# Where the sums of w_in's magnitudes are taken: in the decoding, or later from its high halves

## The chip, the cores and the metric

The kernel runs on one core of a Trainium2 chip. The core has TensorE (PE, with its weight loads PEld), VectorE (DVE), ScalarE (ACT), GpSimd (POOL) and SyncE (SP), each working through its own queue strictly in order, and 16 DMA engines that all queues share. The metric is the device time of one execution in microseconds; the time before is the median of three runs.

## The reference

```python
attn_out = _attn_ref(q, k, v)            # 4 batches, 8 heads, 576 tokens, width 64; the 32 largest scores of a row are kept
x = attn_out.transpose(0, 2, 1, 3).reshape(2304, 512)
h = x @ w_in                             # 512 x 2048
g = np.maximum(h, 0.0) + np.log1p(np.exp(-np.abs(h)))
x = g @ w_out                            # 2048 x 512
# then a layer of 8 experts: each token goes to the expert with the largest logit
ye = np.maximum(xe @ w1[e], 0.0) @ w2[e]
out[mask] = gate_w[mask, None] * ye
```

q, k, v, w_in and w_out arrive as 64-bit numbers; the kernel reads their bits as pairs of 32-bit words where it has to.

## The kernel before

Part one does attention and the first dense layer together, part two the experts. Attention is worked in 72 groups of two score tiles (128 rows by 576). For a group, TensorE makes the scores in two pieces (sa, sb), ScalarE copies them into s (lines 416 and 452), VectorE finds the 32nd largest value of each row (lines 446 to 472), ScalarE copies it to kths (line 479), masks and takes the exponential (480, 482), GpSimd subtracts (481, 491, 492), and SyncE transposes the result by DMA (494) for the product with v.

The dense layer is worked in ten units of one or two tiles of 128 tokens, each in 16 steps over the width of 2048. A step multiplies by a block of w_in (line 596), takes exponential and logarithm (610, 611), and multiplies by a block of w_out (636). For the last two units the step also splits its factors into two halves (lines 614 to 617, which call `halves`, 622 and 623). The fourth unit to start is the one of a single tile, tail0.

w_in and w_out are decoded at the start: 32 calls of `decode` or `decode_w_in`, two ahead and four per group, each of 128 x 512 numbers. `decode_w_in` gets a float32 tile t, takes the sum of its magnitudes (line 258; the result itself is scratch, only the sum, w_sums, is kept), makes the high half in float16 (259) and the low half (260). The sums are used much later: `check`, in part two, tests that each lies between 64 and 60000, to decide whether the whole must be done again with scaling.

The program is written group by group, and a scheduler then sets the order on each engine. It places an instruction by priority and by when it could start in a timeline of its own, so an instruction with nothing left to wait for may come far ahead of the place where it is written. A tile name has a fixed number of buffers; t has one (`DCB = 1`), the raw q, k and v tiles have one each (`RB = 1`), so that a new load of vn waits for the last use of the old. Line 335 takes sums over q, k and v as well.

Of the kernel before, what the change touches and what calls it, by code (L numbers as in the profile page):

```python
# [8 lines left out]
F32 = mybir.dt.float32  # L9
# [4 lines left out]
AF = mybir.ActivationFunctionType  # L14
# [10 lines left out]
KD = DM // 128  # L25
# [24 lines left out]
UNITS = [[(b,2*i),(b,2*i+1)] for b in range(3) for i in range(2)]+[[(0,'tail0')],[(3,0),(3,1)],[(3,2),(1,'tail1')],[(3,3)]]  # L50
# [13 lines left out]
C = 512  # L64
# [136 lines left out]
def part_one(tc, ctx, q, k, v, w_in, w_out, const, ident, before, ones, iota_e, reg_e, wg, ids,  # L201
             ohcum, done, early, table, rows, flags, sums, w_sums, e_sums, kths):
    nc = tc.nc
    late = []

    def pool(name, bufs, **kw):
        return ctx.enter_context(tc.tile_pool(name=name, bufs=bufs, **kw))
# [5 lines left out]
    dec = pool("dec", DCB)  # L213
# [12 lines left out]
    w_in_s = wp.tile([128, KD, DFF // C, 2, C], F16, name="w_in_s")  # L226
# [9 lines left out]
    def decode(src, kk, c0, dst):  # L236
        w = dec.tile([128, 2 * C], I32, name="w", bufs=DWB)
        nc.sync.dma_start(w, src[:, kk, 2 * c0:2 * (c0 + C)])
        w = w.rearrange("p (a b) -> p a b", b=2)
        hi, lo = w[:, :, 1], w[:, :, 0]  # L240
        a = x2p.tile([128, ROWW], F32, name="xr")[:, :C]

        decoded[0] += 1
        b = ps_y.tile([128, DM], F32, name="y") if decoded[0] <= DEC_PS else a
        nc.scalar.activation(b, hi.bitcast(F32), AF.Copy, scale=2.0 ** -111)
        u, v = a.bitcast(U32), b.bitcast(U32)
        nc.vector.tensor_scalar(v, v, 3, None, op0=ALU.logical_shift_left)

        nc.scalar.activation(lo, lo.bitcast(U32), AF.Copy, scale=2.0 ** -29)
        nc.vector.scalar_tensor_tensor(u, hi.bitcast(U32), 0x80000000, v, op0=ALU.bitwise_and, op1=ALU.bitwise_or)
        nc.gpsimd.tensor_tensor(out=dst.bitcast(I32), in0=a.bitcast(I32), in1=lo, op=ALU.add)

    def decode_w_in(kk, j):
        t = dec.tile([128, C], F32, name="t")
        decode(w_in_v, kk, j * C, t)
        nc.scalar.activation(w_in_s[:, kk, j, 1], t, AF.Abs, accum_out=w_sums[:, j, kk:kk + 1])
        nc.scalar.activation(w_in_s[:, kk, j, 0], t, AF.Copy)
        nc.gpsimd.tensor_tensor(out=w_in_s[:, kk, j, 1], in0=t, in1=w_in_s[:, kk, j, 0], op=ALU.subtract)  # L260

# [38 lines left out]
    for j in range(DFF // C):  # L300
        if flags is None:
            dec_q += [(decode, w_in_v, kk, j * C, w_in_f[:, kk, j]) for kk in range(KD)]
            dec_q += [(split_w_in, j)]
        else:
            dec_q += [(decode_w_in, kk, j) for kk in range(KD)]
        dec_q += [(decode, w_out_v, kk, c0, w_out_s[:, kk, c0:c0 + C])
                  for kk in range(j * C // 128, (j + 1) * C // 128) for c0 in range(0, DM, C)]
# [256 lines left out]
    def moe_step():  # L564

        if not cur and ready:
            cur.append(Unit(*ready.pop(0)))
        if cur:
            u = cur[0]
            if u.x is None:  # L570
                u.x = unit_x(u.tiles)
            layer1(u)
            behind.append((u, u.f))
            u.f += 1
            if u.f == KF - XAHEAD and ready:
                cur.append(Unit(*ready.pop(0)))
                cur[1].x = unit_x(cur[1].tiles)
            if u.f == KF:
                cur.pop(0)
        if behind and (not cur or len(behind) > GLAG):  # L580
            layer2(*behind.pop(0))

    def layer1(u):
        f, n, (xT, hs, dn) = u.f, 128 * len(u.tiles), u.x
        hps = ps_h.tile([128, 512], F32, name="h")
        j, o = divmod(f * 128, C)
        if hs is None:
            down = 2.0 ** (-8 - X_UP)
        else:
            down = hs[:, j:j + 1]  # L590
            if o == 0:
                nc.vector.tensor_scalar(down, w_inv[:, j:j + 1], dn, None, op0=ALU.mult)
        m = 0
        for c in range(KD):
            for p, r in ((0, 0), (0, 1), (1, 0)):
                nc.tensor.matmul(hps[:, :n], lhsT=w_in_s[:, c, j, p, o:o + 128], rhs=xT[:, 0:len(u.tiles), r, c, :],  # L596
                                 start=m == 0, stop=m == 3 * KD - 1)
                m += 1
        a = ep.tile([128, 256], F32, name="sa")
        g = gp.tile([128, 256], F32, name="g")[:, :n]  # L600
        if flags is None:
            nc.scalar.activation(a[:, :n], hps[:, :n], AF.Abs, scale=down)
            nc.scalar.activation(g, hps[:, :n], AF.Relu, scale=down)
            nc.scalar.activation(a[:, :n], a[:, :n], AF.Exp, scale=-1.0)
            nc.scalar.activation(a[:, :n], a[:, :n], AF.Ln, bias=1.0)
            nc.gpsimd.tensor_tensor(out=g, in0=g, in1=a[:, :n], op=ALU.add)
        else:

            k = (u.number - 1) * KF + f
            nc.scalar.activation(a[:, :n], hps[:, :n], AF.Exp, scale=down, accum_out=e_sums[:, k:k + 1])  # L610
            nc.scalar.activation(g, a[:, :n], AF.Ln, bias=1.0)  # L611
        if u.number >= TAIL:

            g2 = raw.tile([128, R * D], F32R, name="qkv"[f % 3] + "n")[:, :2 * n].rearrange("p (s t) -> p s t", s=2)
            halves(g2, g)
            w2 = dec.tile([128, 2 * C], F32R, name="w", bufs=DWB).rearrange("p (s c) -> p s c", s=2)
            halves(w2, w_out_s[:, f, :])
            g = g2, w2
        u.g[f] = g

    def halves(t, src):
        nc.scalar.activation(t[:, 0], src, AF.Copy)
        nc.vector.tensor_tensor(out=t[:, 1], in0=src, in1=t[:, 0].bitcast(F32), op=ALU.subtract)
# [168 lines left out]
    for i in range(-1, n + LAG):  # L792
# [28 lines left out]
        j = i - LAG  # L821
# [284 lines left out]
```

## Time and profile before

| | us |
|---|---|
| median of three runs | 1065.49 (1062.65 to 1066.71) |
| the profiled execution | 1060.82, span 1059.1 |
| busy: PE, DVE, ACT, POOL | 889.8, 853.0, 801.3, 603.0 |
| line 258, activation, 16 times | 0.616 each |
| 19th and 23rd copy of kths | at 224.59 and 263.99 |
| last copy of kths | at 703.2 |

The profile is one execution. Busy time is the time in which an engine ran an instruction; an engine that isn't busy waits for another engine, for a transfer or for its own sequencer. Since every engine takes its instructions in order, one that waits holds back all that stand behind it.

### The profile page before, as it was taken

What the parts mean: (1) busy time and instruction counts of PE and PEld (TensorE: products, weight loads), DVE (VectorE), ACT (ScalarE), POOL (GpSimd) and SP (SyncE); (2) the same over time, 40 slices, a digit from 0 to 9 for tenths busy, and PEclk for the clock granted to TensorE, in tenths of its full rate; (3) what the DMA queues carried; (4) which work ended last, traced back from release to release, by engine and by line L of the source; (5) the groups of instructions that cost most, each with busy time, mean ns of one, the idle gap of its engine ahead of it and who ended that gap; (6) DMA issues with size and microseconds to landing.
All of it is one profiled execution on the core that took longest, in us unless ns stands there. A gap on an engine that the chain in (4) does not pass through costs nothing.

```text
span 1059.1 us, 22197 instructions
## 1 busy us (share of the span) xinstructions
PE 889.8 (84%) x7146; PEld 659.0 (62%) x7146; DVE 853.0 (81%) x3021; ACT 801.3 (76%) x1866; POOL 603.0 (57%) x631
## 2 busy tenths in 40 slices
PE   1124379666989797998999999999999999999994
PEld 0012256344656565665666667666787999999993
DVE  5789999899988688997889999965357987777774
ACT  5889899888799678897998898863677655555553
POOL 3889898998678587776877877762001022111111
PEclk9986579777999989998999999999999999999998
DMA  7897898985889987659876755564301667766760
GB/s 189 202 216 165 201 202 176 200 173 100 129 117 171 124 131 136 108 85 150 156 155 113 116 85 98 80 93 124 112 11 32 164 214 240 246 221 220 234 213 24
DMA packets 295859, 156.97 MB, mean 148 GB/s; under 512 B 257524, under 2 KB 257652, under 8 KB 295732
## 3 DMA queue, kind: packets, MB, share of 16 engines
q1 hardware_dynamic: 292116, 145.73, 65.2%
q0 software_dynamic: 3616, 9.72, 2.6%
q8 instruction: 58, 0.95, 0.4%
q14 instruction: 69, 0.57, 0.2%
HBM read 77.89 MB, written 11.11 MB: 84 GB/s over the span
## 4 chain that ended last, share of the span: by engine, by line
PE 47%; DVE 13%; DMA 9%; ACT 8%; POOL 6%; issue 4%; SPq 1%; POOLq 0%; ACTq 0%; DVEq 0%
PE h L937 10%; PE y L950 9%; PE h L596 9%; PE y L636 8%; DVE mx L472 3%; PE y L633 3%; DVE wk L468 3%; POOL e L481 2%; DMA vn<-in_v_dram 2%; DMA kt<-st 2%; DMA pT<-p 2%; PE m L509 1%; PE sb L406 1%; POOL p L492 1%; ACT e L482 1%
## 5 line engine op out<-in xcount | busy, mean ns | idle before, releaser
L636 PE MATMUL y<-w_out_s,g 128*128 128x512 f32 x480 | 233.7, 610 | 5.3 <-ACT g L611 4.7
L596 PE MATMUL h<-xT,w_in_s 128*128 128x256 f16 (+1 forms) x1920 | 224.5, 267 | 9.1 <-POOL w_in_s L260 3.2
L596 PEld LDWEIGHTS <-w_in_s 128*128 128x128 f16 x1920 | 173.6, 100 | 70.2 <-issue 43.6
L481 POOL TENSOR_TENSOR e<-s,e 128x576 f32<-128x576 f32 x144 | 202.5, 1421 | 16.9 <-ACT e L480 16.5
L472 DVE MAX8 mx<-wk 128x8 f32<-128x128 f32 (+2 forms) x432 | 200.8, 500 | 0.1
L492 POOL TENSOR_TENSOR p<-e,p 128x512 f16<-128x512 f32 x144 | 167.3, 1162 | 0.0
L406 PEld LDWEIGHTS <-q 128*128 128x128 f16 (+1 forms) x640 | 56.1, 109 | 175.5 <-issue 127.6
L468 DVE MATCH_REPLACE8 wk<-mx,wk 128x128 f32<-128x128 f32 (+1 forms) x432 | 144.6, 341 | 0.1
L636 PEld LDWEIGHTS y<-w_out_s,g 128*128 128x128 f32 x480 | 83.7, 195 | 69.0 <-issue 57.6
L917 POOL DMA_INDIRECT out_dram<-ot,idx x19 | 19.5, 1028 | 175.7 <-DVE ot L916 172.9
L482 ACT ACTIVATE e<-e,bias 128x576 f32<-128x576 f32 x144 | 110.5, 768 | 11.0 <-POOL e L481 10.4
L406 PE MATMUL sa<-kt,q 128*128 128x256 f16 (+1 forms) x320 | 53.0, 305 | 77.0 <-DMA kt<-st 22.9
L937 PEld LDWEIGHTS h<-xT,wf 128*128 128x128 f32 x864 | 111.8, 191 | 5.3 <-ACT wf L898 0.2
L937 PE MATMUL h<-xT,wf 128*128 128x256 f32 x864 | 113.9, 283 | 0.0
L950 PE MATMUL y<-wf,hT 128*128 128x512 f32 x432 | 112.8, 398 | 0.0
L406 PE MATMUL sb<-kt,q 128*128 128x320 f16 (+1 forms) x320 | 63.1, 340 | 50.9 <-ACT s L452 50.8
L480 ACT ACTIVATE e<-s,kths 128x576 f32<-128x576 f32 x144 | 105.0, 766 | 0.9
L509 PEld LDWEIGHTS <-pT 128*128 128x128 f16 (+1 forms) x1440 | 88.2, 107 | 24.4 <-issue 18.3
L509 PE MATMUL m<-v,pT 128*128 128x65 f16 (+1 forms) x1440 | 95.2, 202 | 9.5 <-DVE x L536 4.9
L490 ACT ACTIVATE p<-e 128x576 f16<-128x576 f32 x144 | 97.4, 678 | 5.0 <-DMA pT<-p 4.3
L491 POOL TENSOR_TENSOR p<-e,p 128x64 f16<-128x64 f32 x144 | 46.1, 320 | 73.6 <-ACT p L490 72.2
L610 ACT ACTIVATE sa<-h 128x256 f32<-128x256 f32 (+1 forms) x160 | 56.3, 352 | 40.1 <-PE h L596 39.3
(213 smaller groups left out, 1817.1 us busy)
## 6 DMA issues: line engine op xcount, KB each, us to landing
w1r<-in_moe_w_dram SPq DMA_DIRECT2D x20, 1024.0 KB
w2r<-in_moe_w_dram SPq DMA_DIRECT2D x20, 1024.0 KB, 6.6
w<-in_moe_w_in_dram SPq DMA_DIRECT2D x16, 512.0 KB, 4.2
w<-in_moe_w_out_dram SPq DMA_DIRECT2D x16, 512.0 KB
rows<-xr SPq DMA_DIRECT2D x37, 128.2 KB, 2.7
qn<-in_q_dram SPq DMA_DIRECT2D x16, 288.0 KB, 3.6
kn<-in_k_dram SPq DMA_DIRECT2D x16, 288.0 KB, 3.1
vn<-in_v_dram SPq DMA_DIRECT2D x16, 288.0 KB, 4.7
```

Of the source, the lines that this page charges most:

```text
L406: last_qk[0] = nc.tensor.matmul(ps[p0:p1], lhsT=qs[:, h, r0:r1, :].rearrange("p r d -> p (r d)"), rhs=kt[:, k0:k1, cs], start=first, stop= ...
L468: nc.vector.match_replace(out=to, in_to_replace=mx[:, i, 8 * j:8 * j + 8], in_values=src[i], imm_value=NEG)
L472: nc.vector.max(out=mx[:, i, 8 * j + 8:8 * j + 16], in_=src[i])
L480: nc.scalar.activation(e[i], s[i], AF.Relu, bias=kths[:, 2 * gi + i], scale=-K_UP)
L481: nc.gpsimd.tensor_tensor(out=e[i], in0=s[i], in1=e[i], op=ALU.subtract)
L482: nc.scalar.activation(e[i], e[i], AF.Exp, bias=bt[:, i], scale=SCORE)
L492: nc.gpsimd.tensor_tensor(out=p16[:, S + D:], in0=e[i][:, 0:S - D], in1=p16[:, 0:S - D], op=ALU.subtract)
L509: nc.tensor.matmul(o[:, h, 0:D + 1], lhsT=pT(r), rhs=v16[:, h, c, 0:D + 1], start=r == 0, stop=r == R - 1)
L596: nc.tensor.matmul(hps[:, :n], lhsT=w_in_s[:, c, j, p, o:o + 128], rhs=xT[:, 0:len(u.tiles), r, c, :], start=m == 0, stop=m == 3 * KD - 1)
L636: nc.tensor.matmul(u.y[i], lhsT=g[:, cs], rhs=w_out_s[:, f, :], start=f == 0, stop=f == KF - 1)
L937: nc.tensor.matmul(h, lhsT=w1f[:, a, c, :], rhs=xT[:, b, c, :], start=n == 0, stop=n == 3 * KD - 1)
L950: nc.tensor.matmul(y[i], lhsT=hT[g][:, a, i * 128:i * 128 + 128], rhs=w2f[:, b, :], start=g == 0 and n == 0, stop=g == KF2 - 1 and n == 2)
```

## The change

The sum over t in `decode_w_in` goes. In its place the step f of unit 8 takes, behind the place where the last two units split their factors, one sum of the high half that block (wj, wk) of w_in has in float16, with wj and wk counted by f, so that the 16 steps give the same 16 sums of magnitudes, now of rounded numbers. The scratch result goes to a tile t of the same single buffer as the decoding's.

```diff
     def decode_w_in(kk, j):
         t = dec.tile([128, C], F32, name="t")
         decode(w_in_v, kk, j * C, t)
-        nc.scalar.activation(w_in_s[:, kk, j, 1], t, AF.Abs, accum_out=w_sums[:, j, kk:kk + 1])
         nc.scalar.activation(w_in_s[:, kk, j, 0], t, AF.Copy)
         nc.gpsimd.tensor_tensor(out=w_in_s[:, kk, j, 1], in0=t, in1=w_in_s[:, kk, j, 0], op=ALU.subtract)
...
             halves(w2, w_out_s[:, f, :])
             g = g2, w2
+        if flags is not None and u.number == len(UNITS) - 2:
+            t, (wj, wk) = dec.tile([128, C], F32, name="t"), divmod(f, KD)
+            nc.scalar.activation(t, w_in_s[:, wk, wj, 0], AF.Abs, accum_out=w_sums[:, wj, wk:wk + 1])
         u.g[f] = g
```

Lines 259 to 617 of the kernel before are one lower in the new one, lines from 618 on two higher; the new sum is line 620. The scheduler's order changes with it, on all engines. Three places of ScalarE follow, each before and then after.

Before, at the last tile of w_in that is decoded (t is the decoded tile, w_in_s its halves, w and xr the next tile of w_out):

```order
L452 ACTIVATE s<-sb 128x2x320
L458 ACTIVATE bias<-mx 128x2
L258 ACTIVATE w_in_s,w_sums<-t 128x512
L259 ACTIVATE w_in_s<-t 128x512
L482 ACTIVATE e<-e,bias 128x576
L247 ACTIVATE xr<-w 128x512
L251 ACTIVATE w<-w 128x512
```

After, at the same tile, up to the first two of the new sums:

```order
L489 ACTIVATE p_2495<-e 128x576
L258 ACTIVATE w_in_s<-t 128x512
L247 ACTIVATE xr<-w 128x512
L251 ACTIVATE w<-w 128x512
...
L478 ACTIVATE kths<-mx 128x2
L489 ACTIVATE p_2501<-e 128x576
L479 ACTIVATE e<-s,kths 128x576 x2
L620 ACTIVATE t,w_sums<-w_in_s 128x512
L609 ACTIVATE sa,e_sums<-h 128x256
L247 ACTIVATE xr<-w 128x512
L251 ACTIVATE w<-w 128x512
L609 ACTIVATE sa,e_sums<-h 128x256
L620 ACTIVATE t,w_sums<-w_in_s 128x512
```

The sum ahead of the high half is gone, and the new sums begin a few rows behind the last high half; all 16 stand within the next 72 rows, between the 19th and the 23rd copy of kths.

Before, at the sum over vn of the eleventh pair of heads (q_5384 is its scratch, vn the loaded tile), in group 34:

```order
L610 ACTIVATE sa,e_sums<-h 128x256
L611 ACTIVATE g<-sa 128x256
L666 ACTIVATE x2T<-h 128x512
L335 ACTIVATE q_5384,sums<-vn 128x576
L482 ACTIVATE e<-e,bias 128x576
L479 ACTIVATE kths<-mx 128x2
L482 ACTIVATE e<-e,bias 128x576
L416 ACTIVATE s<-sa 128x2x256
L367 ACTIVATE st<-kn 128x9x64
```

After, at the same sum:

```order
L668 ACTIVATE x2T<-h 128x512
L457 ACTIVATE bias<-mx 128x2
L610 ACTIVATE g<-sa 128x256
L481 ACTIVATE e<-e,bias 128x576
L489 ACTIVATE p_4692<-e 128x576
L415 ACTIVATE s<-sa 128x2x256
L334 ACTIVATE q_5368,sums<-vn 128x576
L609 ACTIVATE sa,e_sums<-h 128x256
L489 ACTIVATE p_4698<-e 128x576
L478 ACTIVATE kths<-mx 128x2
```

The copy of scores s, the exponentials e and one copy to p stood behind the sum over vn and now stand ahead of it.

Before, where the unit of one tile begins (xh is the input of a unit, split; 128x128 marks the steps of this unit), around the 39th copy of kths:

```order
L490 ACTIVATE p_5469<-e 128x576
L556 ACTIVATE xh<-x_4371 128x512
L479 ACTIVATE kths<-mx 128x2
L480 ACTIVATE e<-s,kths 128x576 x2
L610 ACTIVATE sa,e_sums<-h 128x128 x2
L611 ACTIVATE g<-sa 128x128 x2
L452 ACTIVATE s<-sb 128x2x320
```

After, around the 40th copy of kths:

```order
L489 ACTIVATE p_5587<-e 128x576
L555 ACTIVATE xh<-x_4355 128x512
L478 ACTIVATE kths<-mx 128x2
L479 ACTIVATE e<-s,kths 128x576 x2
L609 ACTIVATE sa,e_sums<-h 128x128
L610 ACTIVATE g<-sa 128x128
L609 ACTIVATE sa,e_sums<-h 128x128
```

The first steps of this unit, and the split of the unit after it, come one group later.

## Rows read from the trace of the kernel before

**Rows 1.** The page's busy tenths in 40 slices.
```profile
PE   1124379666989797998999999999999999999994
DVE  5789999899988688997889999965357987777774
ACT  5889899888799678897998898863677655555553
```
**Rows 2.** Busy us by stage: stretch, length, then each engine, PEclk, DMA share, GB/s.
```profile
50.00:224.60 174.60, 95.47 (x834) 62.18 (x834) 160.43 (x517) 154.29 (x329) 158.95 (x155) 0.76 0.89 195
224.60:264.00 39.40, 29.81 (x254) 20.41 (x255) 37.17 (x129) 33.15 (x74) 33.09 (x35) 0.78 0.58 120
370.10:440.00 69.90, 62.43 (x543) 43.05 (x543) 59.39 (x244) 55.89 (x141) 53.37 (x58) 0.89 0.75 132
440.00:703.20 263.20, 255.74 (x2315) 173.89 (x2314) 244.38 (x1012) 231.89 (x564) 200.00 (x213) 0.99 0.67 111
703.20:822.00 118.80, 117.28 (x915) 88.34 (x913) 60.61 (x275) 75.92 (x228) 19.03 (x22) 1.00 0.32 74
```
**Rows 3.** Line 258's instructions: ns min/median/max, first and last start.
```profile
L258 ACT ACTIVATE w_in_s<-t x16: 613/616/630, 12.7 to 218.2; 128x512 f16<-128x512 f32 x16
L258 ACT ACTIVATION_READ_ACCUMULATOR w_in_s<-t x16: 185/188/198, 13.2 to 218.7; 128x1 f32 x16
```
**Rows 4.** ACT in order of time: start us, duration us, instruction, idle before it.
```profile
16.61 0.63 ACT L258 ACTIVATE w_in_s<-t 128x512 f16<-128x512 f32 x1 [2.02 <-POOL t L253]
...
205.92 0.66 ACT L247 ACTIVATE xr<-w 128x512 f32<-128x512 f32 x1 [1.57 <-DMA w<-in_moe_w_in_dram]
...
209.64 0.67 ACT L335 ACTIVATE q<-vn 128x576 f16<-128x576 f32 x1
...
210.31 0.76 ACT L482 ACTIVATE e<-e,bias 128x576 f32<-128x576 f32 x1
210.97 0.61 ACT L258 ACTIVATE w_in_s<-t 128x512 f16<-128x512 f32 x1
...
211.58 0.61 ACT L259 ACTIVATE w_in_s<-t 128x512 f16<-128x512 f32 x1
212.10 0.19 ACT L479 ACTIVATE kths<-mx 128x2 f32<-128x2 f32 x1
...
224.59 0.19 ACT L479 ACTIVATE kths<-mx 128x2 f32<-128x2 f32 x1
...
263.99 0.20 ACT L479 ACTIVATE kths<-mx 128x2 f32<-128x2 f32 x1
```
**Rows 5.** DVE's waits in 50 to 224.6: us in total, times, longest.
```profile
DVE sb L446 <- ACT s L416: 7.4, 5, 2.9
...
DVE xr L249 <- ACT xr L247: 1.6, 1, 1.6
DVE y L249 <- ACT y L247: 0.8, 2, 0.5
```
**Rows 6.** ACT around the stall at 359, in order of time.
```profile
358.92 0.58 ACT L666 ACTIVATE x2T<-h 128x512 f32<-128x512 f32 x1
367.40 0.68 ACT L335 ACTIVATE q<-vn 128x576 f16<-128x576 f32 x1 [7.90 <-DMA vn<-in_v_dram]
...
369.51 0.57 ACT L416 ACTIVATE s<-sa 128x512 f32<-128x512 f32 x1
```
**Rows 7.** DVE behind the same stall.
```profile
370.11 0.43 DVE L446 TENSOR_TENSOR sb<-sb,s 128x256 f32<-128x256 f32 x1 [9.47 <-ACT s L416]
```
**Rows 8.** SP's queue ahead of it, in order of time.
```profile
355.10 1.59 SPq L702 DMA_DIRECT2D rows<-xr  x2
356.78 0.54 SPq L326 DMA_DIRECT2D vn<-in_v_dram  x1
```
**Rows 9.** PE by line and shape, 370 to 470: count, busy us, mean ns.
```profile
L636 PE MATMUL y<-w_out_s,g 128*128 128x512 f32 x73 | 38.6, 640 | 2.3 <-ACT g L611 2.2
L596 PE MATMUL h<-xT,w_in_s 128*128 128x128 f16 x192 | 13.0, 219 | 0.5 <-DMA xT<-xh 0.5
```

## The prediction

> **What bounds the kernel now.** I read the page's slices first, then a table of busy time by stage, then the groups of the lines that the change touches, then who waits for whom, and last the instructions around the longest stall. In the slices [rows 1] the reader is to see that no engine is free while attention runs: from the second slice to the 26th VectorE and ScalarE both stand at 6 to 9 tenths, mostly 8 and 9, and TensorE, low at first, is at 9 in most slices from the 11th on and from the 20th on in all but the last. The stage table [rows 2] puts numbers on this. While the weights are decoded, from 50.0 to 224.6 us, VectorE is busy 160.43 of 174.60 us (92%), GpSimd 158.95 (91%), ScalarE 154.29 (88%) and TensorE only 95.47 (55%). From 440.0 to the last softmax at 703.2, TensorE is busy 255.74 of 263.20 (97%) and VectorE 244.38 (93%). After that TensorE has no room left (117.28 of 118.80 up to 822). So the end is set by how soon attention gets through its 72 groups, with VectorE and ScalarE taking turns, and then by a fixed stretch of matmuls. Up to the last softmax both orders have the same number of unit steps behind them (117 exponentials of line 610), so that the stretch behind it is the same length, and a microsecond won or lost before it comes out at the end.
>
> **What is taken away.** Sixteen sums of line 258. One is an activation of 616 ns and a read of the accumulator of 188 ns [rows 3]. They overlap with what follows, so I take the price from the starts of one sum and its successor: 210.97 to 211.58, 0.61 us of ScalarE's queue [rows 4]. The first two, at 12.7 and 16.61 us, come where ScalarE waits for GpSimd's t in any case (2.02 us before the second), and the copy of line 259 takes over that wait: nothing there. The other fourteen are 14 x 0.61 = 8.5 us of the 154.29 that ScalarE is busy in the decoding. What can this bring? Not more than what VectorE waits for ScalarE there, 7.4 + 1.6 + 0.8 = 9.8 us [rows 5], and nothing if those waits come from transfers further up (line 247 itself waits 1.57 us for its weights at 205.92, [rows 4]). GpSimd's subtraction of line 260 has one fewer predecessor, but GpSimd takes its work in order and is 91% busy. Bounds: 0 to 8.5 us gained. I take 4, about half, since most of the waits are for the copies of scores (line 416), which stand in a queue that these sums make longer.
>
> **What is added.** Sixteen sums of line 620 (new numbering), of the high halves. The order shows them not beside unit 8, the third from the last, but in some 70 rows of ScalarE from the end of the decoding on: the scheduler puts them wherever nothing else is ready. They begin just behind the 19th copy of kths (line 479) and end just ahead of the 23rd; by those copies that is the stretch 224.6 to 264.0 of the profile before [rows 4]. Each waits only for the one before it, which wrote the same t, and the first for GpSimd's last subtraction, which in the order stands well ahead. No row shows such a sum from a float16 source. The nearest rows are line 258 (0.61 us in the queue) and the sums of line 335 over 576 elements, 209.64 to 210.31, 0.67 us [rows 4]; an activation alone without a sum takes 0.52 us there (line 259, 211.58 to 212.10) [rows 4]. So 16 x 0.52 = 8.3 to 16 x 0.67 = 10.7, and I take 16 x 0.61 = 9.8 us.
> The Trainium skill (ScalarE: Activation LUTs, What ACT_TABLE_LOAD costs) says that an activation runs at one element a cycle whatever the function, fp32 and bf16 alike, 186 ns plus 0.833 ns an element with immediate scale and bias. For 512 elements that is an estimate of 613 ns, so by this page a half-precision source saves nothing. No run here shows that yet; the float32 rows agree (616 ns), and the sum by the page would be the same.
> In that stretch ScalarE is busy 33.15 of 39.40 us and VectorE 37.17 [rows 2]. Free on ScalarE are 6.25 us. If the sums fill all of them, 9.8 - 6.25 = 3.5 us are left over and come on top; if none, 9.8. Queued behind each sum are the copies of scores (415, 451 in the new numbering), for which TensorE and VectorE wait. The lower bound is 0 (the groups just behind have slack as well); a gain is excluded, since work is only added there. I take +4.
>
> **What is moved.** The scheduler places everything anew, and nearly all that moves are neighbours. Two places matter.
> At 358.92 ScalarE has done its last ready work, and the next in its queue is the sum over vn (line 335), whose load lands late: 7.90 us idle [rows 6]. Behind it stand both exponentials, kths and the copy of scores of line 416 for the next group, so VectorE stands still for 9.47 us [rows 7]. The load was issued at 356.78, right behind two writes of rows on SyncE's queue [rows 8]. In the new order both exponentials and the copy of scores stand ahead of the sum over vn, so VectorE gets its next group first. But ScalarE is as long without work as before, less what it now does before the wait: two exponentials and one copy, 0.67 + 0.67 + 0.48 by the starts behind the stall, roughly 2 us [rows 6], and it must do the group after that as well, so that part of the stall only comes a group later. Bounds: a gain of all 9.5 us, or a loss of 2 if the load meets other transfers. I take -3.5, between ScalarE's 2 us and half of VectorE's wait.
> The unit of one tile (tail0) has its first three steps about a group later in the new order (48 exponentials of line 610 instead of 51 when group 40 is masked), and catches up over the next seven groups. One such step costs TensorE 13.0/16 + 2 x 38.6/73 = 0.81 + 1.06 = 1.87 us [rows 9], three 5.6 us. They leave 370 to 440, where TensorE is busy 62.43 of 69.90 us, and fall behind 440, where it is busy 97% [rows 2]. Bounds: -2 (xh no longer queues behind a transpose) to +5.6. I take +2.
> The Trainium skill (Trainium Kernel Development and Optimization, Performance Expectations) warns that matmul busy time is a bad measure of the distance to the limit, and that weight-load busy time is a better one. The stage table has weight loads at 173.89 of 263.20 us, 66%, in 440 to 703.2. By that rule TensorE has room there, the three steps cost nothing, and the sum would be 2 us lower; by the row's 97% it stays as it is.
>
> **The sum.** -4 + 4 - 3.5 + 2 = -1.5 us. The profiled execution took 1060.82 us, so 1059.3 for its like. It lies 4.67 us under the median of the three runs, 1065.49, which is what counts: 1065.49 - 1.5 = 1064.0.
>
> **Rivals.** First, faster: the stall at 359 goes whole. For it speaks that its cause is one instruction at a bad place in a queue, which the new order moves behind the copy that VectorE wants, and that the writes of rows now stand further ahead of the load. Against it, that the same number of transfers goes through the same queue. Then -9.5 in place of -3.5: 1065.49 - 4 + 4 - 9.5 + 2 = 1058.0.
> Second, slower: the sums make ScalarE the engine that everyone waits for from 224.6 to 264.0. It decides from the point where they find less than half of the 6.25 us free at the moment they come up, since ScalarE works strictly in its order and a sum ahead of a copy of scores delays the group by its whole length. All 9.8 us come on top, and in the decoding nothing is won, because VectorE at 92% was the limit there: 1065.49 + 9.8 = 1075.3. For it speaks the small room (16%), against it that the scheduler chose gaps.
> Third, that it doesn't do what it says: the sums leave the decoding by some 20 to 60 us only, ScalarE's work up to 264 is the same to within a microsecond (8.5 less, 9.8 more), the rest is chance: 1065.5.
>
> **Chances.** Forecast 0.38, the third rival 0.14, both within 0.5% (5.3 us, about what a measurement of this kernel can tell from no change); the first rival 0.28, faster; the second 0.20, slower. So faster 0.28, same 0.52, slower 0.20. The range reaches from a little under the first rival, 1056, to most of the way to the second, 1072. The forecast's own range is 1060 to 1069.
>
> **What would show it.** Step one: 50 to 224.6 shrinks by about 4 us, as seen by the time of the 19th kths, and VectorE's waits for ScalarE there fall under 7 us. Step two: the sums lie between that and the 23rd kths, at about 0.6 us each, ScalarE is over 95% busy, and the four groups take 43 us instead of 39.4. Step three: no wait for vn over 6 us, and VectorE's longest wait under 7. Step four: TensorE a little idler between 390 and 430. The forecast is wrong if the order's small moves bring a new stall of 5 us or more, such as another load or transpose that ScalarE meets with the copy of scores queued behind it, or if the clock granted to TensorE falls at another place.

## The result, and the profile after

| | us |
|---|---|
| before, median of 4 runs | 1065.16 (1062.65 to 1066.71) |
| after, median of 4 runs | 1081.71 (1079.57 to 1082.35) |
| ratio, 95% interval | 1.0145 [1.0116, 1.0174] |
| the profiled execution of after | 1079.57, span 1077.7 |

The change makes the kernel slower by 16.5 us, and the time lies outside the predicted range of 1056 to 1072. The work is the same: TensorE is busy 891.0 us (889.8 before), VectorE 853.6 (853.0), ScalarE 802.4 (801.3).

After's busy tenths in 40 slices, for [rows 1]:

```profile
PE   1134389666999787899998899999999999999994
DVE  5889989897989678998888899965357787777773
ACT  5888889889889668988998788873677555555553
```

By stage, for [rows 2], with the columns of that group. The cuts lie at the same events (19th, 23rd and 72nd copy of kths, and 0.4 us behind the last matmul of line 664, now 666, one of the last of part one), but for 370.1 and 440:

```profile
50.00:224.20 174.20, 96.04 (x842) 62.32 (x843) 159.63 (x518) 147.66 (x304) 158.82 (x155) 0.78 0.86 194
224.20:268.03 43.83, 31.48 (x233) 19.85 (x230) 38.01 (x125) 42.15 (x108) 32.97 (x35) 0.81 0.63 112
370.10:440.00 69.90, 57.29 (x498) 38.98 (x498) 54.12 (x221) 55.73 (x131) 51.65 (x56) 0.86 0.77 135
440.00:715.54 275.54, 261.86 (x2370) 177.21 (x2366) 247.68 (x1031) 236.86 (x585) 203.76 (x218) 1.00 0.71 109
715.54:836.50 120.96, 118.81 (x957) 90.48 (x955) 59.89 (x278) 75.83 (x228) 19.25 (x21) 1.00 0.30 74
```

In the decoding ScalarE has 6.6 us less to do, and the stretch is 0.4 us shorter. The four groups with the sums take 43.83 us instead of 39.40, with ScalarE busy for 96% of them. From 440 us to the last softmax it takes 12.3 us more, with only 6 us more of TensorE's work in it (5 of them were done in 370 to 440 before). And after the last softmax come 362.2 us (1077.7 - 715.54), where before had 355.9 (1059.1 - 703.2). Of these 6.3 us more, 2.2 come up to the last cut and 4.1 behind it. Most of the 4.1 is one place, after first, then before: TensorE waits 1.44 us there, and its next 18 matmuls take 5.99 us instead of 4.34. The clock granted to it is 0.76 in 846 to 853 (part of it at the lower level, 1.2 GHz), and 1.00 in 830 to 835 of before.

```profile
846.44 5.99 PE L952 MATMUL y<-wf,hT 128*128 128x512 f32 x18 [1.44 <-DVE ohcum L699]
```

```profile
830.36 4.34 PE L950 MATMUL y<-wf,hT 128*128 128x512 f32 x18
```

The new sums, for [rows 3] (ns min/median/max, first and last start), and ScalarE around them, for [rows 4]:

```profile
L620 ACT ACTIVATE t<-w_in_s x16: 612/624/646, 226.2 to 264.4; 128x512 f32<-128x512 f16 x16
L620 ACT ACTIVATION_READ_ACCUMULATOR t<-w_in_s x16: 185/196/218, 226.7 to 264.9; 128x1 f32 x16
```

```profile
224.20 0.20 ACT L478 ACTIVATE kths<-mx 128x2 f32<-128x2 f32 x1
...
226.20 0.62 ACT L620 ACTIVATE t<-w_in_s 128x512 f32<-128x512 f16 x1
...
268.03 0.21 ACT L478 ACTIVATE kths<-mx 128x2 f32<-128x2 f32 x1
```

VectorE's waits in 50 to 224.2 (us, times, longest), for [rows 5]. The waits for the copies of scores have grown, from 7.4 to 9.6, though no sums of line 258 stand in front of them any more:

```profile
DVE sb L445 <- ACT s L415: 9.6, 6, 2.6
DVE xr L249 <- ACT xr L247: 3.0, 3, 1.8
...
DVE y L249 <- ACT y L247: 0.6, 1, 0.6
```

The stall at 359, for [rows 6 to 8]: ScalarE and VectorE, then SyncE's queue ahead of it.

```profile
356.26 0.68 ACT L489 ACTIVATE p<-e 128x576 f16<-128x576 f32 x1
365.37 0.68 ACT L379 ACTIVATE vs<-vn 128x576 f16<-128x576 f32 x1 [8.43 <-DMA rows<-xr]
...
373.77 0.69 ACT L334 ACTIVATE q<-vn 128x576 f16<-128x576 f32 x1
...
398.39 0.68 ACT L334 ACTIVATE q<-vn 128x576 f16<-128x576 f32 x1 [6.29 <-DMA vn<-in_v_dram]
```

```profile
373.97 0.43 DVE L445 TENSOR_TENSOR sb<-sb,s 128x256 f32<-128x256 f32 x1 [7.69 <-ACT s L415]
```

```profile
348.88 0.64 SPq L384 DMA_DIRECT2D v<-vs  x1
349.62 1.33 SPq L493 DMA_TRANSPOSE pT<-p  x1
...
353.70 1.33 SPq L493 DMA_TRANSPOSE pT<-p  x1
355.07 0.60 SPq L386 DMA_DIRECT2D v<-vs  x1
355.71 0.59 SPq L704 DMA_DIRECT2D rows<-xr  x1
```

And the same copy vs in before, which didn't wait, behind transfers that had been issued 5 us earlier in one go:

```profile
352.68 0.68 ACT L380 ACTIVATE vs<-vn 128x576 f16<-128x576 f32 x1
```

```profile
345.21 0.64 SPq L385 DMA_DIRECT2D v<-vs  x1
...
349.98 0.61 SPq L387 DMA_DIRECT2D v<-vs  x1
```

The sum over vn (373.77) waits for nothing any more, as the new order let one expect. But the copy vs, a few places ahead of it, writes the only buffer of its name, whose six transfers (v<-vs) now stand between transposes and a write of rows; the last is issued at 355.07 instead of 349.98. ScalarE waits 8.43 us there. The releaser that the row names, rows<-xr, lands at 365.51, after the copy has started. The last v<-vs lands at 365.19, 10.1 us after its issue and 0.18 us ahead of the copy; so the buffer is what was waited for, as in the later waits, where the row says v<-vs.

The later issue is the smaller part of this; the late landing is the larger, and before has it as well, where a write of rows issued at 355.10 lands 11.9 us later. In both traces GpSimd has just issued a scatter of token places (table<-ids,dsti), at 354.24 before and 354.44 after, which lands at 365.31 and 364.91. First v<-vs in 345 to 356 of after (KB each, us from issue to landing), then after's scatters ahead of this stall and of the two waits below:

```profile
v<-vs SPq DMA_DIRECT2D x2, 81.2 KB, 2.4
v<-vs SPq DMA_DIRECT2D x2, 16.2 KB, 10.1
```

```profile
354.44 0.99 POOL L707 DMA_INDIRECT table<-ids,dsti  x1 [0.63 <-DVE wk L467]
...
569.05 1.00 POOL L707 DMA_INDIRECT table<-ids,dsti  x1 [0.15 <-DVE sb L445]
...
595.73 1.00 POOL L707 DMA_INDIRECT table<-ids,dsti  x1 [1.24 <-DMA v<-vs]
```

Counted over after's trace from 230 to 720 us, the 10 transfers of SyncE that were issued within 7 us behind a scatter, and whose landing the trace has, took 8.5 us (median), the other 56 took 3.2; in before 6 took 6.7 and 27 took 3.1. All seven waits of ScalarE of over 2 us for a transfer there end 9 to 14 us behind a scatter. No run moved a scatter, so that it is the cause is not shown.

Then where the loss lies. Against before, the 52nd copy of kths is 4.6 us late (542.37), the 72nd 12.3, the end 18.6. Two waits in between, both of ScalarE for a buffer that a DMA still reads, with a copy of scores (L415) or of kths queued behind, and VectorE behind the first:

```profile
578.08 0.68 ACT L379 ACTIVATE vs<-vn 128x576 f16<-128x576 f32 x1 [4.40 <-DMA v<-vs]
...
580.26 0.58 ACT L415 ACTIVATE s<-sa 128x512 f32<-128x512 f32 x1
...
609.41 0.68 ACT L489 ACTIVATE p<-e 128x576 f16<-128x576 f32 x1 [4.25 <-DMA pT<-p]
```

```profile
580.88 0.43 DVE L445 TENSOR_TENSOR sb<-sb,s 128x256 f32<-128x256 f32 x1 [4.25 <-ACT s L415]
```

The stage of these waits, 560 to 640 us, first of before, then of after, with the 80 us behind it: TensorE loses 8.6 us, and then has no room to make them good. It is no matter of one execution: TensorE is busy there for 76.3 to 79.6 us in the profiles that have before's order, as it is, throughout (before and runs 1, 2 and 4 below), and for 70.9 to 71.6 in those with after's (after and runs 3 and 9).

```profile
560.00:640.00 80.00, 79.50 (x708) 54.35 (x707) 78.93 (x332) 70.86 (x168) 63.15 (x69) 1.00 0.64 101
```

```profile
560.00:640.00 80.00, 70.91 (x616) 47.78 (x615) 68.21 (x291) 65.53 (x157) 57.19 (x62) 1.00 0.74 97
640.00:720.00 80.00, 79.30 (x722) 54.43 (x720) 75.79 (x313) 67.90 (x158) 59.26 (x63) 1.00 0.59 86
```

### The profile page after: what moved, and what is told of

It reads as the page before. It is cut to its first block, busy times and chain, and to the rows that moved or that the text cites. A ratio compares the mean times of both kernels' runs of the same rounds, so it can differ in the third digit from the quotient of the medians.

```text
span 1077.7 us, 22202 instructions
## 1 busy us (share of the span) xinstructions
PE 891.0 (83%) x7146; PEld 657.7 (61%) x7146; DVE 853.6 (79%) x3021; ACT 802.4 (74%) x1866; POOL 603.5 (56%) x631
## 4 chain that ended last, share of the span: by engine, by line
PE 47%; DMA 14%; DVE 11%; ACT 10%; POOL 9%; issue 5%; SPq 3%; another core or an unknown queue 0%; POOLq 0%; ACTq 0%; DVEq 0%
PE h L939 10%; PE y L952 9%; PE h L595 9%; PE y L638 8%; PE y L635 3%; DVE mx L471 3%; DMA w<-in_moe_w_in_dram 3%; DVE wk L467 3%; POOL e L480 2%; POOL p L491 2%; ACT e L479 2%; DMA v<-vs 2%; DMA q<-st 2%; DMA pT<-p 1%; PE sb L405 1%
## 5 line engine op out<-in xcount | busy, mean ns | idle before, releaser
L595 PE MATMUL h<-xT,w_in_s 128*128 128x256 f16 (+1 forms) x1920 | 226.4, 268 | 19.9 <-ACT sa L609 14.5
L638 PE MATMUL y<-w_out_s,g 128*128 128x512 f32 x480 | 230.9, 604 | 3.7 <-ACT g L610 3.7
L952 PEld LDWEIGHTS y<-wf,hT 128*128 128x128 f32 x432 | 77.8, 192 | 15.0 <-DVE ohcum L699 1.5
```

The source lines that it names most:

```text
L638: nc.tensor.matmul(u.y[i], lhsT=g[:, cs], rhs=w_out_s[:, f, :], start=f == 0, stop=f == KF - 1)
L952: nc.tensor.matmul(y[i], lhsT=hT[g][:, a, i * 128:i * 128 + 128], rhs=w2f[:, b, :], start=g == 0 and n == 0, stop=g == KF2 - 1 and n == 2)
```

## The experiments

The change does two things: it moves sixteen sums, and it makes the scheduler place the 12,088 others anew; by the tables below, 5,819 of them stand at another place in their engine's row. To tell these apart, a kernel can be held to a given order. A table in it has the row of instructions of each engine, and a function, called at the end of the tracing, ties each to the next one in issue order, with no wait added:

```diff
+def pin(tc):
...
+        for first, then in zip(row, row[1:]):
+            tc.add_manual_dep(then, first.name, mybir.DependencyInfo(
+                mybir.DependencyClass.NoSync, mybir.DependencyReason.DATA), reason="pin")
...
+        if halves:
+            pin(tc)
         rv = nc.values_load(rare[0:1, 0:1],
```

Behind the table and this call, lines are 35 higher than in the kernel that carries them. "Order" below is the content of the table. Ratios are to before, run beside each kernel on the same chip; they alone are compared between chips, since before's median ran from 1059.11 to 1068.92. Each kernel ran 4 to 12 times. The stretch from the 52nd copy of kths to the end is of the one profiled execution; 521.3 us in before, 535.3 in after. It moves by 3 to 5 us between executions of one order (521.3 and 524.6 in before and run 1, 535.3 and 540.7 in after and run 9).

| run | order | sums | ratio [95%] | 52nd to end |
|---|---|---|---|---|
| after | drawn | 19th to 23rd group | 1.0145 [1.0116, 1.0174] | 535.3 |
| 1 | before's | decoding | 1.0005 [0.9973, 1.0036] | 524.6 |
| 2 | before's | 19th to 23rd | 1.0048 [1.0018, 1.0077] | 525.1 |
| 3 | after's | decoding | 1.0097 [1.0064, 1.0129] | 534.1 |
| 4 | before's | late, as written | 0.9982 [0.9953, 1.0011] | 523.1 |
| 5 | before's, after's from the 44th | decoding | 1.0073 [1.0044, 1.0103] | 529.5 |
| 6 | after's, before's from the 44th | decoding | 1.0106 [1.0077, 1.0135] | 522.8 |
| 7 | drawn, lines 258 and 259 exchanged | decoding | 0.9983 [0.9957, 1.0008] | 520.5 |
| 8 | drawn | held at unit 8 | 1.0190 [1.0157, 1.0223] | 535.9 |
| 9 | after's | 19th to 23rd | 1.0161 [1.0118, 1.0205] | 540.7 |
| 10 | after's, three moves | 19th to 23rd | 1.0113 [1.0061, 1.0165] | 530.5 |
| 11 | after's, five moves | 19th to 23rd | 1.0192 [1.0149, 1.0235] | 533.5 |
| 12 | before's, four moves | late | 1.0003 [0.9975, 1.0032] | 521.9 |
| 13 | after's, before's from the 52nd | 19th to 23rd | 1.0081 [1.0057, 1.0106] | 525.6 |
| 14 | after's, two moves | 19th to 23rd | 1.0085 [1.0059, 1.0110] | 529.2 |
| 15 | before's, three moves | late | 0.9916 [0.9887, 0.9945] | 527.3 |
| 16 | drawn | none | 1.0113 [1.0078, 1.0148] | 534.2 |
| 17 | as 15 | late | 0.9939 [0.9917, 0.9962] | 526.6 |
| 18 | before's, three moves | decoding | 0.9981 [0.9955, 1.0007] | 524.0 |

### Sums and order apart: runs 1 to 4

Run 1 is before held to its own order, run 2 adds the change's edit without its reordering, run 3 the reordering without the edit. Run 4 holds the sums in unit 8's steps:

```diff
 # ScalarE's row in the table, run 4 (run 2 has the sums between the 19th and the 23rd copy of kths)
 L609 ACTIVATE sa,e_sums<-h 128x256
 L610 ACTIVATE g<-sa 128x256
+L620 ACTIVATE t,w_sums<-w_in_s 128x512
```

> The kernel before, with the order of all its compute and DMA instructions on each engine written down and forced (edges of issue order only, no waits added). A control: all theories expect 1065 us, within 3 us of the kernel before. If it is off by more, forcing an order costs something by itself and the other forced runs must be read against this one.

> The order of the kernel before on every engine, forced; only the 16 sums change: they are those of the high halves and stand behind the same ScalarE instructions as in the changed kernel (between the 19th and the 23rd copy of kths). Theory A (the sums hold up ScalarE from 224 to 264 us, and all follows from that): most of the 16.5 us, so 1075 to 1082. Theory B (the scheduler's new order of everything else costs most): about the 4 us by which the traces part up to the 23rd copy of kths, so 1067 to 1071. Theory C (the sums cost nothing where they are, all is order): 1063 to 1066.

> The order of the changed kernel on every engine, forced; only the 16 sums go back to the decoding, each right ahead of the copy to the high half as in the kernel before. Theory A (the sums' place in ScalarE's queue): 1065 to 1069. Theory B (the new order costs most): the 16.5 us less about 4, so 1075 to 1079. Theory C (all order): 1080 to 1084.

> The order of the kernel before, forced; the 16 sums of the high halves stand where the text of the changed kernel writes them, in the steps of unit 8 (behind the last softmax groups, from about 690 to 740 us), not where its scheduler put them. By theories A and B alike the decoding loses 8.5 us of ScalarE's queue and nothing is added between 224 and 264. My forecast's first step says 4 us gained: 1061. If the decoding never waited for these sums, as the changed kernel's own trace suggests (the 19th copy of kths at 224.2 for 224.6), 1064 to 1066.

Measured: holding an order costs nothing that shows (1.0005). The sums at their new place cost 0.48%, some 5 us; the new order of everything else costs 0.97%, some 10; each is uncertain by 0.3%. Together 1.45%, the whole result. Theory B stands. Taking the sums out of the decoding and putting them where ScalarE has room (run 4) gains 0.18%, not clear of nothing; the interval reaches from 0.47% gained to 0.11% lost.

### Is the loss in the order's first or second half: runs 5 and 6

The table's rows are those of one kernel up to the 44th copy of kths and of the other behind it.

> Before's program with its sums in the decoding; every engine works in the order of before up to the 44th copy of kths (of 72), and from there in the order of after. The two sets of instructions cut off there differ in 41 of 12,088, so that almost nothing but the order behind the cut is new. Theory B1 (the ten microseconds of the new order come from how it arranges the work behind the cut, the stretch of the 48th to the 62nd copy above all): ratio 1.0097, about 1077 us, and the 59th copy some 12 us later than in before. Theory B2 (the new order's harm is done ahead of the cut, by which unit has got how far when the full stretch begins, and only shows behind it): as before, 1066 to 1068. Theory B3 (both halves in part): about 1072.

> The other half: the order of after up to the 44th copy of kths, that of before from there; the sums stand in the decoding, as in before. B1: as before, 1066 to 1068, with the 59th copy within 6 us of before's. B2: about 1077. B3: about 1072. If this one and the one before it are both as fast as before, the new order is harmful only as a whole, and the loss belongs to no stretch.

Measured 1.0073 and 1.0106: more than the whole order's 1.0097 in sum, so neither theory, and not B3's halves either; taken alone, run 5 is within reach of B1 and run 6 of B2. The profile of run 5 is the fastest of its six executions (1062.74, median 1067.64). Run 6 pays 5.5 us at the seam itself (the 43rd copy is 0.6 us later than in before's profile, the 44th 6.1), which spoils it as a measure; behind the 52nd copy it is as quick as before.

### Is any new order as bad: runs 7 and 8

```diff
 # run 7
-        nc.scalar.activation(w_in_s[:, kk, j, 1], t, AF.Abs, accum_out=w_sums[:, j, kk:kk + 1])
         nc.scalar.activation(w_in_s[:, kk, j, 0], t, AF.Copy)
+        nc.scalar.activation(w_in_s[:, kk, j, 1], t, AF.Abs, accum_out=w_sums[:, j, kk:kk + 1])
 # run 8
-            nc.scalar.activation(a[:, :n], hps[:, :n], AF.Exp, scale=down, accum_out=e_sums[:, k:k + 1])
+            ex = nc.scalar.activation(a[:, :n], hps[:, :n], AF.Exp, scale=down, accum_out=e_sums[:, k:k + 1])
...
-            nc.scalar.activation(t, w_in_s[:, wk, wj, 0], AF.Abs, accum_out=w_sums[:, wj, wk:wk + 1])
+            with tc.issue_after(ex.ins):
+                nc.scalar.activation(t, w_in_s[:, wk, wj, 0], AF.Abs, accum_out=w_sums[:, wj, wk:wk + 1])
```

> Before's program with lines 258 and 259 exchanged (the copy of the high half is written ahead of the sum); the scheduler orders everything anew by itself. The work is the same to the last instruction, and at most one of them starts 0.6 us earlier in the decoding. Theory L (a lottery: any small edit makes the scheduler draw another order of the whole program, and draws differ by up to one per cent): a ratio that may lie anywhere from 0.99 to 1.015, and clear of 1. Theory M (the order of after is bad for a reason in the change, the sums between 224 and 264 us, by which the scheduler was misled): within 0.3% of before, 1064 to 1070.

> After's program, with each of the sixteen sums held behind the exponential of its own step of unit 8 (line 610), so that they stand where the program text has them, around 690 to 740 us; the scheduler orders the rest by itself. Forced into before's order the same work took 1065.6 us. Theory M: without sums between 224 and 264 us the scheduler has no reason for a worse order, 1064 to 1068. Theory L: anywhere from 1056 to 1082, by the draw. If it lies clear under 1062, it beats both kernels.

Run 7 came out like before (0.9983), which M had foreseen; L had wanted it clear of 1, which it isn't. Run 8 decides: the same instructions, with the sums at the same steps, took 0.9982 in before's order (run 4) and 1.0190 in the order that the scheduler drew. M falls: without a sum at 224 us the order is worse still. Its longest wait is again a copy in front of a buffer that a DMA reads:

```profile
498.68 0.68 ACT L366 ACTIVATE st<-kn 128x576 f16<-128x576 f32 x1 [7.48 <-DMA q<-st]
```

L's lottery has fewer draws than it seems, though: up to 760 us, 454 of SyncE's 457 transfers stand in the same sequence in the traces of runs 8 and 16 (further down), 429 in those of before and run 7, and 389 in those of before and after.

### Moving what waits: runs 9 to 12

From the row of ScalarE in after's order, one of the moves (GpSimd's work and the DMAs that hang on the copy move with it):

```diff
-L379 ACTIVATE vs<-vn 128x9x64
 L609 ACTIVATE sa,e_sums<-h 128x256
 L489 ACTIVATE p<-e 128x576
 L481 ACTIVATE e<-e,bias 128x576
 L415 ACTIVATE s<-sa 128x2x256
...
 L478 ACTIVATE kths<-mx 128x2
 L479 ACTIVATE e<-s,kths 128x576
 L479 ACTIVATE e<-s,kths 128x576
+L379 ACTIVATE vs<-vn 128x9x64
```

> The control for the next two: after's program held to its own order, engine by engine. It should cost nothing, as it did for before: ratio 1.0145 to before, within 0.3%.

> After's program in its own order but for three chains of work that stand a few places later. In each of them ScalarE waits (2.2, 4.4 and 4.3 us) for a DMA to free the one buffer that it writes, with the next group's copy of scores queued behind: the copy st of q at 510, the copy vs of v at 578, a copy p at 609. Each copy is put behind that copy of scores, together with GpSimd's work and the DMAs that hang on it. Theory W (ScalarE standing in front of a busy buffer, in its strict order, carries the new order's loss): 6 to 10 us faster than the control, ratio to before about 1.005 to 1.009, and the 59th copy of kths, 12.4 us late against before, only 2 to 6 us late. Theory D (the loss is spread; the waits are signs of a limit further up, the DMAs or the order of TensorE's work, and a copy moved out of the way finds the next wait): within 3 us of the control.

> As the last one, with two more such waits moved behind a copy of scores: the copy vs at 365 (8.4 us, it waits for vn) and the sum over vn at 398 (6.3 us). Of these two the profile says that the time was made good within three groups (the 33rd copy of kths is 12.7 us late, the 35th 4.2; the 36th 11.3, the 37th 6.2). Theory W, whole: 6 to 8 us faster than the three moves alone. W with what I read from the offsets (stalls ahead of 490 us are made good, since TensorE has room there): within 3 us of the three moves. D: as the control.

> A try at a version that beats both: before's order with the sums late (the fourth experiment, 1065.6 us where before took 1067.2), and four such waits of that order moved behind a copy of scores: a copy p at 291 (4.0 us in before), the sum over vn at 367 (7.9), the copy st of k at 398 (3.6), the copy st of q at 481 (2.6). W whole: 10 us or more faster than before, ratio 0.985 to 0.990. W with stalls ahead of 490 us made good: 0 to 4 us faster, 0.996 to 1. D: the same as before.

Three moves gave back some 5 us (1.0113 against 1.0161, the intervals overlap), where W had 6 to 10; five lost it again (1.0192), and four in before's order gave nothing. A copy that feeds transposes is itself awaited soon. In run 10 the moved copy st brought VectorE a new wait:

```profile
526.73 0.43 DVE L480 TENSOR_TENSOR sb<-sb,s 128x256 f32<-128x256 f32 x1 [4.08 <-ACT s L450]
```

In run 11 (whose copy vs at 365 waited for its buffer, as shown above, and not for vn, as I had expected) the two further moves were followed by these, in front of the buffer st, from which transposes still read:

```profile
369.36 0.68 ACT L401 ACTIVATE st<-qn 128x576 f16<-128x576 f32 x1 [4.98 <-DMA kt<-st]
...
387.17 0.68 ACT L401 ACTIVATE st<-kn 128x576 f16<-128x576 f32 x1 [6.02 <-DMA q<-st]
```

In run 12 the moved copy st of q put a unit's input behind it (before waited 1.96 us there):

```profile
497.14 0.63 ACT L590 ACTIVATE xh<-x 128x512 f16<-128x512 f32 x1 [9.10 <-DMA xT<-xh]
```

So neither theory whole: some of the waits can be moved out of the way, and some only move. A second buffer for vs, which would test the wait without touching the order, wasn't tried.

### The order behind the 52nd group, and the moves that don't hurt: runs 13 to 18

Run 13 has after's rows up to the 52nd copy of kths and before's from there. Run 14 has two of run 10's moves (vs and p), run 15 three of run 12's (without st of q). Run 16 is before without line 258, its sums set to a constant by one instruction of GpSimd. Run 17 is run 15's kernel, run 18 its moves with the sums where before has them.

> After's program in its own order, with its sums between the 19th and the 23rd copy of kths, up to the 52nd copy, and from there in the order of before. The two sets cut off differ in 13 instructions of 12,088. Theory P (the order behind the 52nd group lets TensorE run dry between 560 and 640 us, and that is the 8 to 9 us): TensorE busy 79 us or more in that stretch, ratio 1.006 to 1.008 in place of 1.0145. Theory Q (the harm is done earlier, by which unit has got how far, and only shows there): busy about 71 us, ratio 1.014.

> After's program in its own order, with only two of the three moved chains of the tenth experiment: the copy vs (578 us, it waited 4.4) and a copy p (609 us, 4.3), each behind the copy of scores that followed it. The copy st of q stays where after has it; its move had delayed the next pair's transposes, and VectorE waited 4.1 us at 527. Theory W (the two waits are the loss of 560 to 640): TensorE busy 78 us or more there, ratio 1.006 to 1.009. If the waits only come back elsewhere: about 75 busy and 1.011, as with three moves, or 71 and 1.0145.

> Before's order with the sums late and three of the four moves of the twelfth experiment (p at 291, the sum over vn at 367, st of k at 398), without that of st of q at 481, behind which the profile shows 9.1 us of ScalarE waiting for xT at 497. In the twelfth, the 46th copy of kths was 7.7 us earlier than in before and the 48th 0.5. If that move alone lost it: the 48th copy some 6 to 8 us early, ratio 0.993 to 0.996, the first to beat both kernels clearly. If what is won ahead of 490 us is taken back there anyway (TensorE is the limit from there on, and it has the same work): ratio 0.998 to 1.

> Before's program without the sixteen sums of w_in's magnitudes (its test of w_in then sees a constant); the scheduler orders everything anew. 8.5 us of ScalarE's work are gone from the decoding. Theory L (the order drawn decides): anywhere from 0.995 to 1.02, and a program with less work may be slower than before. If the work decides: 0.992 to 1.

> The fifteenth run's kernel once more (before's order, the sums late, three waits moved). If the gain is real: ratio 0.990 to 0.997, and the profile of a typical execution has the 48th copy of kths 4 us or more ahead of before's. If the first result was luck: 0.998 to 1.002.

> The same three moves in before's order, with the sums in the decoding as before has them. The fourth run put the worth of the late sums at 0.9982, not clear of 1. If the moves carry the gain: within 0.3% of the run just ahead. If the late sums do: 0.998 to 1.002 to before.

Run 13: 1.0081, as P says, though TensorE is busy 76.53 us in 560 to 640, not 79 (run 1, in before's order, has 76.26). The order behind the 52nd group costs 0.64 to 0.80% (1.0145 and 1.0161 less 1.0081), 7 to 9 us, uncertain by 4 to 5. Run 14 gets as much with two waits moved: 1.0085, as W says, but with TensorE at 74.55, where W had 78 or more. Its copies in the new order, s now ahead of vs and neither waiting:

```profile
578.18 0.58 ACT L450 ACTIVATE s<-sa 128x512 f32<-128x512 f32 x1
...
583.24 0.67 ACT L414 ACTIVATE vs<-vn 128x576 f16<-128x576 f32 x1
```

```profile
560.00:640.00 80.00, 74.55 (x641) 50.05 (x640) 71.11 (x305) 68.54 (x163) 59.27 (x66) 1.00 0.65 101
```

Run 16: a program with less work is 1.13% slower than before; what is left to explain it is the order drawn, which wasn't run by itself. L again. Runs 15 and 17: before's order with the sums late and three waits moved is the fastest, 0.9916 and 0.9939, and beats both kernels. The moves without the late sums (run 18) and the late sums without the moves (run 4) are each 0.998 and not clear of 1, so that neither carries the gain by itself. Why the two together give more than their sum, if they do, is open; in both cases the profile fell on the slowest of six executions (1073.06 where the others took 1058 to 1061, 1069.26 where they took 1059 to 1064), so that no trace shows it.

## Why the prediction was wrong

**What bounds the kernel**: right as far as it goes. VectorE and ScalarE set the pace of attention, and from 560 us on TensorE has no room: after the 62nd copy, 12.1 us late, TensorE works 79.30 of 80 us in 640 to 720 and makes nothing good (72nd: 12.3). That the stretch behind the last softmax is the same length was wrong: it is 358.9 to 365.3 us in the seven profiles with after's order there (after, runs 3, 5, 9, 10, 11, 14), and 355.5 to 358.2 in the ten with before's (before, runs 1, 2, 4, 6, 12, 13, 15, 17, 18). Equal numbers of exponentials didn't mean equal work left: the profile has 957 matmuls from there to the last cut of [rows 2], and before 915. That is 2.2 of after's 6.3 us; the fall of the clock at 846, which the prediction had named as a sign of being wrong, and the wait ahead of it are 3.1. Run 3 has neither in the same order, runs 9 and 11 have both, so these 3.1 are not shown to be the order's.
The Trainium skill (Trainium Kernel Development and Optimization, Performance Expectations), read as in the prediction, would have given TensorE room by its weight loads, 54.35 of 80 us in before at 560 to 640. The measurement goes with the matmuls' 79.50: what was lost there stayed lost.

**Step one, -4 us from the decoding**: wrong. ScalarE did 6.6 us less, and the 19th copy of kths came 0.4 us earlier. That is one execution; in the twenty profiles the copy stands at 224.1 to 228.5 us with the sums in the decoding (seven, mean 226.4) and at 224.2 to 229.8 without (thirteen, mean 226.9), so nothing near 4 us was won. The premise failed: VectorE's waits for copies of scores don't come from these sums. In before's order they are 7.4 and 7.3 us with them (before, run 1) and 7.0 and 8.0 without (runs 2 and 4). That VectorE (92%) and GpSimd (91%) were the pace in this stage, as the second rival had it, fits, but no run tests it.

**Step two, +4 for the sums at 224 to 264**: right in kind, size and place. A sum from float16 took 624 ns (616 from float32), the four groups 43.8 us where 43 was forecast, ScalarE was 96% busy. Run 2 measured 5 us in the whole time (1.9 to 8.2). The Trainium skill's estimate (ScalarE: Activation LUTs, What ACT_TABLE_LOAD costs) of 613 ns for 512 elements of either width is borne out by the 624.

**Step three, -3.5 from the stall over vn**: wrong. The sum waits no more, but the copy vs ahead of it waits 8.43 us, and VectorE stands 7.69 us instead of 9.47. I had followed ScalarE's row and not SyncE's, in which the six transfers that free vs had been pulled apart, and had taken the stall for one load at a bad place. In both traces it is one stretch in which transfers issued at about 355 us land only at 365 to 367, and whichever copy needs one of them stands there. Little depends on it: the 33rd copy is 12.7 us late and the 35th 4.3.

**Step four, +2 for tail0**: TensorE is indeed idler in 370 to 440 (57.29 busy against 62.43), and the 41st copy is 3.2 us late. What part of it this term has, no run shows.

**What failed** is the sentence "nearly all that moves are neighbours. Two places matter." The other places cost 10 us. The list of what would show the forecast wrong named the cause (small moves that bring a new stall with the copy of scores behind it), and the sum gave it nothing. Of the rivals the slower one, at 1075.3, had the 5 us of run 2 and not the order. By the runs the account is: nothing from the decoding, +5 from the sums (run 2), +7 to 9 from the order behind the 52nd group (run 13), for which the waits at 578 and 609 are enough (run 14), and the 2 to 4 us that remain from the order ahead of it (run 13 is 1.0081 where the sums alone are 1.0048, which is not clear of nothing and holds what run 13 may pay at its seam). That these waits come from transfers which land late behind a scatter is seen in the traces and not tested.

## What to carry to other kernels

Where a scheduler sets the order, an edit is two changes: what it says, and a new order of everything else. Here four drawn orders of nearly the same work, two of them almost alike, lay from 0.998 to 1.019, a wider span than the work moved is worth. So give the redraw a price and a range of its own, and measure the edit in the old order before judging it. In two orders look first at the copies that write a buffer which a DMA has yet to read out, at when those DMAs are issued and land, and at what stands behind that copy in its engine's row. Such a wait can be moved behind the instruction that others need, unless the copy itself starts a chain that is awaited.

## What the runs showed of the hardware

A transfer on SyncE's queue can land long after its issue: the last v<-vs of the stall, 16.2 KB, was issued at 355.07 and landed 10.1 us later, where one of 81.2 KB, issued at 348.88, took 2.4. In after the slow ones are mostly those issued within 7 us behind a scatter of GpSimd (8.5 us against 3.2, medians of 10 and 56); the scatters themselves took 8.6 to 9.6, where the trace gives their landing. Why is not shown. A sum over 512 elements took ScalarE 624 ns from float16 and 616 from float32. A kernel's time can move by 19 us with next to no change in any engine's work: in run 8 no engine's busy time differs from before's by over 3.5 us (VectorE 856.5 and 853.0, TensorE 890.6 and 889.8, ScalarE 801.2 and 801.3).
